# Value products of head pairs as quarters of the matmul array, in two banks that VectorE adds, under a new instruction order

## The chip, the cores and the metric

One core of a Trainium2 chip runs the whole program in one launch. The metric is the device time of one execution in microseconds (us). The kernel before takes 504.94 us, the median of three runs (504.84 to 505.65).

## What is computed

The reference, cut to what matters:

```python
# attention: 8 batches, 8 heads, 576 positions, 64 wide; window 128; bias by head
scores = scale * np.matmul(q, k.transpose(0, 1, 3, 2))
mask = (rel >= 0) & (rel < window)                  # rel = query - key
scores = np.where(mask, scores + bias[None], -1e9)
attn = softmax(scores);  attn_out = np.matmul(attn, v)
x = attn_out.transpose(0, 2, 1, 3).reshape(B, S, H * D)   # 512 wide
# four "experts", each a causal attention of its own on x, 64 wide
for e in range(4):
    q, k, v = x @ wq[e], x @ wk[e], x @ wv[e]
    a = softmax(causal(scale * (q @ k.transpose(0, 2, 1))))
    ye = a @ v @ wo[e]
    out += gate_weight(e)[..., None] * ye           # the two best of four by x @ w_gate
```

Only the product of the attention's probabilities with `v` is touched by the change. Because of the window, a key reaches only its own position and the 127 queries behind it.

## The kernel before, in words

The 576 positions are four blocks of 128 (`NQ` = 4, `P` = 128) and a tail of 64 (`TAIL`). The heads go in pairs: 32 pairs `g`, four to a batch, and a pair's results fill 128 partitions, head 0 in the lower 64 (`D` = 64) and head 1 in the upper. The work of one pair is: scores (`attn_s`, `products`), biased row minima on VectorE, exponentials on ScalarE, row sums and the scaling by them (`normalise`, on GpSimd or ScalarE), transposes of the probabilities on TensorE (`attn_t`), and the value product (`attn_pv`, `attn_pv_tail`). The first four pairs go through functions of their own (`half_s`, `half_t`, `half_pv`), which the change leaves as they are; `attn_pv` serves the other 28.

The transposed probabilities of a pair lie in one wide tile `ptT[g]`: keys on partitions, and for key block `c` and head `h` 256 columns, first the queries of the same block, then those of the next. `attn_pv(g, c)` multiplies the 128 keys of block `c` with these 256 columns (128 for the last block), one matmul for each head. A matmul whose weights have 128 rows and 64 columns takes half of the array, so the two heads run side by side. All four blocks add into one PSUM bank `x0`. Then the sum leaves PSUM in two parts, high and low:

```python
act_copy(xh[:, :512], x0, 512)                                  # ScalarE or VectorE, rounds to fp32r
dve_sub(xl[:, :512], x0, xh[:, :512].bitcast(F32), 512)         # VectorE
```

`attn_pv_tail` does the same for the 64 queries of the tail in a second bank `xt`. High and low part are the input `X` of the projections: `vproj` and `qkproj` multiply the four `X` of a batch with the high and low part of the weights, in fp32r on the whole array. The experts' attention (`moe_s`, `moe_t`, `moe_pv`, `moe_wo`) follows with up to a batch of delay. All this is interleaved.

A matmul on plain fp32 data (scores, value products) leaves two records in the trace, one for each of its two passes; fp32r matmuls and transposes leave one.

There are eight PSUM banks (`ps_s`, `ps_t` and `ps_a` are the same eight slots). `place` gives a tile a slot when the order reaches its first use, and frees it behind its last. Some instructions have two engines to choose from: `evac` (ScalarE or VectorE), `rnd` (GpSimd or ScalarE), `ssub` (VectorE or GpSimd).

Nothing is scheduled at run time. The functions only record instructions; `plan` then puts them in the order that the packed string `ORDER` holds (a place in the recorded list for each step, and which engine where there is a choice). Every engine works through its own part of that order from front to back, and waits at an instruction whose inputs or buffers are not ready. All instructions are issued by one line of the program, so the profile's rows are told apart by tiles: `ps` is a PSUM bank, `w` any of the SBUF slots, `wx` an `X`, `vt` the values, `WH`/`WL` the projection weights, `idt` the identity of a transpose.

Of the kernel before, what the change touches and what calls it, by code (L numbers as in the profile page):

```python
# [10 lines left out]
F32 = mybir.dt.float32  # L11
# [31 lines left out]
    "BWvdWi@@%Xnb!-wKJqVxw!OT_YgR2ElQ)qZaEB;BsZB33VcYTT6STbmv+d-p)GN4yYJ@6KY!)?`P1MqJ5^u(;*-Xnl5qv|=$U#8^b-)zmOs%^Qw63aUc"
    "m6ZVVA|YY{cmd|X2w+G6YgVAY(n{t)FnD>NLkGHrEV6}@5A+W70@~dJFTSOHga5up5Rw3wazMr~?-a(mge>7+?lSnQD$Bb}8a_5X5k&r2gc6W10>Iq8Z"
    "UzHrg{eRP4*ckaZ@&doVzCP*+wA6SgRW@(ZY+ea49J|-?x&U!{XOSe{&H{$R!iB(v>sn)pv4%NTT(p=A9+v{YaAW=7`%0Cj0H2g%|Pzu=Gc9uxsw^jvF"
    "Sz~cr6w%@&>JOu_V790C#+{0deut3fJHmKackDW9XWDss8DITToLnean`4+Q#b+scoIY{?fYD(ev^X>W|X--Sa<t(3EMm#b)qD4yT~!(}kvNK)@zKjK~"
    "|FDArC7#+T-K;ySX@(z^MaLc3|nUtqJ#7Fo>r2mkNEfBk_3O=@}LZmXlQ+?(gs-m4W1zasA*6v6yzP00j6_xi}4Js24ufzf#y8SPx<=zRsxYgXs{d{?l"
    "*ezf3k(^u63Tm_HzS#A%J7+kA>iaNnO#Ot9j*bkNEl?YE*)dJ`=+eaQR9|UOr47XUGUa^*x+|pQLgIl^=qn-hx&GuNdhCzR0P30;icXi>gUVsMNvLJ1J"
    "sCNHo4c1oxw4hsr>&y6T4X4J>&e)O~p;i!n#d&M_h1!wi)a0_-cet^lQP9(cbwk8xF~$Z+BQZl04@tZ5_&<x)bq~Gsu9{7<Kihr(U*8l4-T&~9WEMdE!"
    "-l54{pufoMelFA?T1EyrUoblD7dLF6ii=x_W&#z2rbZ;i-IA=QJZE@Ljb1H0ElJ92(?T^a<jjzV}B3MMh1$LeJ*RBIeGnh3Y71-;?uN=;+#>}lbN1r@X"  # L50
    "l3Brd7>P$9Zanut9@&019D94p~=0ZUHPsKna83{HH6YCszmDfm3m6-23o<davfY8_?Ab(1xLClV@21bkIr&WThlKJ-B=D<;#~YX~i+nk=lb7zmi^9bov"
    "+YzEH3trr$g`+A`@EM$X>+tJJKc^2JYI7R!wSsgGLLp#es7w|v!c=dDNTnYiO+5c~4slOWh$3eJsfSV$%8Wc~bp`;OLdbD6j-Lq+9RKC8*Kk<?;H(KzA"
# [194 lines left out]
def attn_moe_kernel(ctx, tc, hd, rd, vd, wall, wo, mk, tb, tm, mt, ident, out):  # L247
# [1034 lines left out]
```

## Time and profile before

| | |
|---|---|
| median of three runs | 504.94 us |
| the profiled execution's own time | 505.44 us |
| its span, first to last instruction | 503.6 us |
| TensorE busy / weight loads | 498.3 us (99%) / 428.3 us (85%) |
| VectorE, ScalarE, GpSimd busy | 420.0 us (83%), 352.5 us (70%), 178.2 us (35%) |
| DMA queue q1, share of the 16 engines | 31.8% |

The profiled execution lasts 1.8 us longer than its span. It is 0.5 us above the median of the three runs. "Busy" is the time in which at least one instruction of the engine is under way. Matmuls overlap each other, so TensorE's 99% does not say that each of its matmuls runs at the best rate; what a matmul costs is read from the distance of starts in the timeline.

### The profile page before, as it was taken

What the parts mean: (1) busy time and instruction counts of PE and PEld (TensorE: products, weight loads), DVE (VectorE), ACT (ScalarE), POOL (GpSimd) and SP (SyncE); (2) the same over time, 40 slices, a digit from 0 to 9 for tenths busy, and PEclk for the clock granted to TensorE, in tenths of its full rate; (3) what the DMA queues carried; (4) which work ended last, traced back from release to release, by engine and by line L of the source; (5) the groups of instructions that cost most, each with busy time, mean ns of one, the idle gap of its engine ahead of it and who ended that gap; (6) DMA issues with size and microseconds to landing.
All of it is one profiled execution on the core that took longest, in us unless ns stands there. A gap on an engine that the chain in (4) does not pass through costs nothing.

```text
span 503.6 us, 15006 instructions
## 1 busy us (share of the span) xinstructions
PE 498.3 (99%) x5212; PEld 428.3 (85%) x5212; DVE 420.0 (83%) x1879; ACT 352.5 (70%) x1313; POOL 178.2 (35%) x403
## 2 busy tenths in 40 slices
PE   8999999999999999999999999999999999999997
PEld 6888889897889879798887978989789897799775
DVE  5999999989995898968979899697988869845853
ACT  4969977887868478673797869556585878455852
POOL 3812425160715115252230603408152055105440
PEclk9999999999999999999999999999999999999999
DMA  7994440243107043054242312710344300200033
GB/s 202 281 233 123 105 109 3 65 110 99 38 17 197 13 122 97 6 147 123 68 114 72 81 53 61 214 33 1 87 134 143 81 2 1 91 1 1 2 105 126
DMA packets 29851, 44.83 MB, mean 89 GB/s; under 512 B 9424, under 2 KB 15824, under 8 KB 29776
## 3 DMA queue, kind: packets, MB, share of 16 engines
q1 hardware_dynamic: 29040, 43.42, 31.8%
q8 instruction: 41, 0.67, 0.6%
q10 hardware_dynamic: 736, 0.46, 0.4%
q14 instruction: 34, 0.28, 0.2%
HBM read 34.42 MB, written 9.44 MB: 87 GB/s over the span
## 4 chain that ended last, share of the span: by engine, by line
PE 98%; DMA 1%; SPq 0%; DVE 0%; issue 0%
PE ps L1194 98%; DMA w<-in_hd 1%; SPq L1194 0%; DVE w L1194 0%
## 5 line engine op out<-in xcount | busy, mean ns | idle before, releaser
L1194 POOL TENSOR_SCALAR w<-w,mr,w 128x256 f32<-128x256 f32 (+3 forms) x128 | 76.3, 606 | 111.4 <-DVE mr L1194 43.9
L1194 PE MATMUL ps<-wx,WH 128*128 128x288 f32 (+2 forms) x512 | 112.2, 300 | 0.0
L1194 ACT ACTIVATE w<-w,nm 128x128 f32<-128x128 f32 x252 | 98.6, 394 | 15.9 <-DVE nm L1194 14.8
L1194 ACT COPY w<-ps 128x512 f32<-128x512 f32 (+3 forms) x132 | 62.4, 499 | 41.5 <-PE ps L1194 32.1
L1194 POOL TENSOR_SCALAR w<-w,r 128x128 f32<-128x128 f32 x156 | 55.9, 369 | 92.7 <-DVE r L1194 29.7
L1194 PEld LDWEIGHTS ps<-wx,WH 128*128 128x128 f32 x512 | 83.2, 189 | 2.4 <-issue 0.9
L1194 ACT ACTIVATE w<-w,mnm 128x256 f32<-128x256 f32 (+3 forms) x128 | 70.8, 555 | 15.1 <-DVE mnm L1194 9.5
L1194 PE MATMUL ps<-idt,w 128*128 128x128 f32 x608 | 80.2, 276 | 0.0
L1194 DVE CUSTOM_DVE_ANT_0 w<-ps,tbt 128x128 f32<-128x128 f32 x288 | 72.5, 284 | 5.2 <-PE ps L1194 3.5
L1194 DVE TENSOR_TENSOR w<-ps,tmt 128x1024 f32<-128x1024 f32 (+2 forms) x96 | 71.6, 772 | 2.6 <-PE ps L1194 1.3
L1194 PEld LDWEIGHTS ps<-idt,w 128*128 128x128 f32 x608 | 69.0, 141 | 4.5 <-issue 1.3
L1194 PE MATMUL ps<-wx,WL 128*128 128x288 f32 (+2 forms) x256 | 71.8, 297 | 0.0
L1194 PE MATMUL ps<-w,vt 128*64 128x256 f32 (+2 forms) x784 | 66.1, 309 | 0.0
L1194 DVE COPY w<-ps 128x256 f32<-128x256 f32 (+3 forms) x90 | 47.7, 544 | 18.8 <-PE ps L1194 18.1
L1194 PE MATMUL ps<-WH,wx 128*128 128x260 f32 x288 | 62.3, 284 | 0.0
L1194 PEld LDWEIGHTS ps<-w,vt 128*64 128x64 f32 x784 | 44.2, 137 | 21.1 <-issue 3.5
L1194 PE MATMUL ps<-w 64*64 64x192 f32 (+2 forms) x1256 | 57.7, 313 | 0.3 <-DMA w<-in_hd 0.2
L1194 PEld LDWEIGHTS ps<-w 64*64 64x64 f32 (+1 forms) x1256 | 43.8, 138 | 10.3 <-issue 2.3
L1194 PE MATMUL ps<-w,w 128*64 128x64 f32 (+4 forms) x576 | 51.6, 318 | 0.0
L1194 DVE CUSTOM_DVE_ANT_0 w<-ps,mtt 128x384 f32<-128x384 f32 (+2 forms) x96 | 50.3, 551 | 0.9 <-PE ps L1194 0.5
L1194 DVE COPY_PREDICATED ps<-mkt,ps 128x256 f32<-128x256 int32 (+2 forms) x160 | 49.7, 329 | 1.1 <-PE ps L1194 0.5
L1194 ACT ACTIVATE w<-w,r 128x128 f32<-128x128 f32 x132 | 46.2, 395 | 5.3 <-DVE r L1194 5.1
(102 smaller groups left out, 933.1 us busy)
## 6 DMA issues: line engine op xcount, KB each, us to landing
w<-in_hd SPq DMA_DIRECT2D x56, 288.0 KB, 4.5
vt<-in_vd SPq DMA_DIRECT2D x28, 320.0 KB, 3.8
out<-w SPq DMA_DIRECT2D x31, 256.0 KB, 2.9
w<-in_hd SPq DMA_DIRECT2D x14, 128.0 KB, 4.0
w<-in_hd SPq DMA_DIRECT2D x56, 32.0 KB, 3.7
w<-in_wall SPq DMA_DIRECT2D x4, 386.0 KB, 5.3
out<-w SPq DMA_DIRECT2D x8, 128.0 KB, 2.4
vt<-in_vd SPq DMA_DIRECT2D x4, 192.0 KB, 4.1
```

The source lines that it names most:

```text
L1194: getattr(getattr(tc.nc, e), m)(*a, **k)
```

## The change

The value product of the 28 pairs is cut once more, by keys. `half(dst, q0, y, c, f, n)` takes the 64 lower (`y` = 0) or upper (`y` = 1) keys of block `c` and issues one matmul for each head, with weights of 64 rows and 64 columns, a quarter of the array. The 64 lower keys reach the first 192 of the 256 columns, the 64 upper keys the last 192, so each matmul has 192 columns in place of 256. Lower keys add into bank `xa`, upper keys into bank `ya`, and the tail's lower keys into a third bank `ta`; the tail's upper keys go into the first 64 columns of `ya`, which no other product uses.

The two banks are put together behind TensorE: `evac` copies `xa` to a tile `tmp` in SBUF, VectorE adds columns 64 to 511 of `ya` to it, `rnd` makes the high part from `tmp`, and `ssub` the low part, with no PSUM operand any more. For the tail, `evac` copies `ta` to a small tile and VectorE adds `ya`'s first 64 columns and writes the sum back to `ta`; `tail_out` is then what stood at the end of `attn_pv_tail`.

The string `ORDER` is replaced as a whole.

```diff
 ORDER = (
-    "c-obC4OAo7m1b4FD^<~|ZpoHnDG?qNix}AugDtXRjS|>EMjDG)$^jopAb|vCVJtFW!y0BG0Wa({4tOC0HXMTod0`C+%t8WVaOeciX%a|a3>$O;4xG@FW"
...
+    "c-obC0azr*b>?)}>#p9N*3L*X5@XF+j20wDfdm}Jh8Sc>zy}t{@C6dc!6&%D9oQfb7Mwr^8@wRF24ryHyf~~44#;5bN~{Go*bu=9EO0=9c=-%5_#lA`Y"
...
-    def attn_pv(g, c):
-        b, p = divmod(g, NP_)
-        vt = prepped[g][3]
-        if c == 0:
-            xacc[g] = ps_a.tile([P, 512], F32, tag="x" if K["X"] else "a", name=f"x{g}", bufs=K["X"] or K["A"])
-        x0 = xacc[g]
-        n = 2 * P if c < NQ - 1 else P
-        pc = ptT[g]
-        for h in range(2):
-            nc.tensor.matmul(
-                x0[D * h : D * h + D, P * c : P * c + n], vt[:, c, D * h : D * h + D],
-                pc[:, 4 * P * c + 2 * P * h : 4 * P * c + 2 * P * h + n],
-                start=(c == 0), stop=True, skip_group_check=True,
-            )
-        if c == NQ - 1:
-            X = xp.tile([P, 2 * S + TAIL], F32R, tag="xh", name=f"xh{g}")
-            xh, xl = X[:, :S], X[:, S + TAIL :]
-            xT[g] = (xh, xl)
-            xX[g] = X
-            act_copy(xh[:, :512], x0, 512)
-            dve_sub(xl[:, :512], x0, xh[:, :512].bitcast(F32), 512)
-            del xacc[g]
+    def attn_pv(g):
+        vt, pc = prepped[g][3], ptT[g]
+        xa, ya, ta = (ps_a.tile([P, 512], F32, tag="x", name=f"{n}{g}") for n in ("x", "y", "xt"))
+
+        def half(dst, q0, y, c, f, n, start=False):
+            r = slice(D * y, D * y + D)
+            for h in range(2):
+                m = 4 * P * c + 2 * P * h + f
+                nc.tensor.matmul(
+                    dst[D * h : D * h + D, q0 : q0 + n], vt[r, c, D * h : D * h + D], pc[r, m : m + n],
+                    start=start, stop=True, skip_group_check=True,
+                )
+
+        for c in range(NQ - 1):
+            half(xa, P * c, 0, c, 0, 3 * D, c == 0)
+            half(ya, P * c + D, 1, c, D, 3 * D, c == 0)
+        c = NQ - 1
+        half(xa, P * c, 0, c, 0, P)
+        half(ya, 0, 1, c, P, TAIL)
+        half(ta, 0, 0, c, P, TAIL, True)
+        half(ya, P * c + D, 1, c, D, D)
+        half(ta, 0, 0, NQ, 0, TAIL)
+        tmp = big2.tile([P, DM], F32, tag="xs", name=f"xs{g}")
+        evac(tmp, xa)
+        nc.vector.tensor_tensor(tmp[:, D:], tmp[:, D:], ya[:, D:], add)
+        X = xp.tile([P, 2 * S + TAIL], F32R, tag="xh", name=f"xh{g}")
+        xh, xl = X[:, :S], X[:, S + TAIL :]
+        xT[g], xX[g] = (xh, xl), X
+        rnd(xh[:, : NQ * P], tmp)
+        ssub(xl[:, : NQ * P], tmp, xh[:, : NQ * P].bitcast(F32))
+        tt = p2.tile([P, TAIL], F32, tag="xq", name=f"xq{g}")
+        evac(tt, ta[:, :TAIL])
+        nc.vector.tensor_tensor(ta[:, :TAIL], tt, ya[:, :TAIL], add)
+        tail_out(g, ta)
...
     def run(g):
         n = len(nc.ops)
-        for c in range(NQ):
-            attn_pv(g, c)
...
-        attn_pv_tail(g)
+        attn_pv(g)
```

What the new order does is shown at three places around pair 7, the last of its batch. The rows are in program order of one engine; `x2` counts matmuls that follow each other with equal text, and the sizes are those of the result (partitions x columns).

TensorE, the value product of pair 7 (`vt7`), before:

```order
L1194 MATMUL ps4_73<-w103_93,vt7_157 64x256 x6
L1194 MATMUL ps7_76<-w103_93,vt7_157 64x64 x2
L1194 MATMUL ps4_73<-w103_93,vt7_157 64x128 x2
L1194 MATMUL ps7_76<-w103_93,vt7_157 64x64 x2
L1194 MATMUL ps0_69<-w50_82 64x192 x2
L1194 MATMUL ps2_71<-w50_82 64x192 x2
```

and now:

```order
L1206 MATMUL ps5_74<-w103_93,vt7_158 64x192 x2
L1206 MATMUL ps4_73<-w103_93,vt7_158 64x192 x2
L1206 MATMUL ps5_74<-w103_93,vt7_158 64x128 x2
L1206 MATMUL ps4_73<-w103_93,vt7_158 64x64 x2
L1206 MATMUL ps0_69<-w103_93,vt7_158 64x64 x2
L1206 MATMUL ps4_73<-w103_93,vt7_158 64x64 x2
L1206 MATMUL ps0_69<-w103_93,vt7_158 64x64 x2
L1206 MATMUL ps2_71<-w57_89 64x128 x2
L1206 MATMUL ps7_76<-w57_89 64x128 x2
```

The first two of these rows are the last of three equal pairs. Twelve matmuls in two banks became 22 in three (`xa` is `ps5`, `ya` is `ps4`, `ta` is `ps0`); behind them the scores of another pair follow at both times.

TensorE, the first projection that reads the `X` of pair 7 (`wx3` before), before, ten rows on from the last row of the product:

```order
L1194 MATMUL ps0_69<-w50_82 64x192 x2
L1194 MATMUL ps2_71<-w50_82 64x192 x2
L1194 MATMUL ps3_72<-wx0_77,WH_109 128x288
L1194 MATMUL ps4_73<-wx4_81,WH_109 128x288 x2
L1194 MATMUL ps4_73<-wx4_81,WL_110 128x288
L1194 MATMUL ps4_73<-wx1_78,WH_109 128x288
L1194 MATMUL ps3_72<-wx0_77,WL_110 128x288
L1194 MATMUL ps3_72<-wx3_80,WH_109 128x288 x2
```

and now (pair 7 is `wx2`):

```order
L1206 MATMUL ps5_74<-w57_89 64x192 x2
L1206 MATMUL ps4_73<-wx4_81,WH_109 128x288
L1206 MATMUL ps6_75<-wx1_78,WH_109 128x288
L1206 MATMUL ps4_73<-wx4_81,WH_109 128x288
L1206 MATMUL ps4_73<-wx4_81,WL_110 128x288
L1206 MATMUL ps4_73<-wx0_77,WH_109 128x288 x2
L1206 MATMUL ps4_73<-wx0_77,WL_110 128x288
L1206 MATMUL ps4_73<-wx1_78,WH_109 128x288
L1206 MATMUL ps6_75<-wx1_78,WL_110 128x288
L1206 MATMUL ps4_73<-wx1_78,WH_109 128x288
L1206 MATMUL ps6_75<-wx2_79,WH_109 128x288
```

Between the scores and the first read of pair 7 there stood six projection matmuls; now there are ten.

GpSimd, the same stretch of the program, before:

```order
L1194 TENSOR_SCALAR QJm_118<-QLm_122 64x64
L1194 TENSOR_TENSOR w0_145<-ex_117,ws0_170 128x5x4
L1194 TENSOR_SCALAR w53_85<-w53_85,mr0_0_0_171,w0_145 128x256
L1194 TENSOR_SCALAR MPL0_119<-MPL0_119,mr0_0_2_174 128x576
L1194 TENSOR_SCALAR QJm_118<-QHm_121 64x64
```

and now:

```order
L1206 TENSOR_SCALAR QJm_118<-QLm_122 64x64
L1206 TENSOR_SCALAR w54_86<-w54_86,r7_0_167 128x128 x2
L1206 TENSOR_TENSOR wx0_77<-w22_96,wx0_77 128x512
L1206 TENSOR_SCALAR wx1_78<-w23_97 128x512
L1206 TENSOR_TENSOR ex_117<-lg0_144,mx0_172 128x5x4
L1206 TENSOR_TENSOR wx1_78<-w23_97,wx1_78 128x512
L1206 TENSOR_TENSOR w0_145<-ex_117,ws0_173 128x5x4
L1206 TENSOR_SCALAR QJm_118<-QHm_121 64x64
L1206 TENSOR_SCALAR w50_82<-w50_82,mr0_0_0_174,w0_145 128x384
L1206 TENSOR_SCALAR w50_82<-w50_82,mr0_0_0_174,w0_145 128x128
L1206 TENSOR_TENSOR wx2_79<-w24_98,wx2_79 128x512
```

The subtractions (`TENSOR_TENSOR wx`) and some of the roundings (`TENSOR_SCALAR wx`) of the `X` now stand on GpSimd between the gates and the scaling of the probabilities; pair 7's low part is the last row.

## Rows read from the trace of the kernel before

**Rows 1.** The page: busy times, the granted clock, and the chain that ended last.
```profile
PE 498.3 (99%) x5212; PEld 428.3 (85%) x5212; DVE 420.0 (83%) x1879; ACT 352.5 (70%) x1313; POOL 178.2 (35%) x403
...
PEclk9999999999999999999999999999999999999999
...
PE ps L1194 98%; DMA w<-in_hd 1%; SPq L1194 0%; DVE w L1194 0%
```

**Rows 2.** Waits of the weight loads: releaser: us in total, times, longest us.
```profile
PEld ps L1194 <- issue: 22.2, 101, 0.5
```

**Rows 3.** Timeline of TensorE, value products as halves (start, us, ..., xrecords).
```profile
419.22 1.03 PE L1194 MATMUL ps<-w,vt 128*64 128x256 f32 x8
420.08 0.60 PE L1194 MATMUL ps<-w,w 128*64 128x256 f32 x4
...
89.78 0.39 PE L1194 MATMUL ps<-w,vt 128*64 128x128 f32 x4
90.00 0.49 PE L1194 MATMUL ps<-w,w 128*64 128x384 f32 x2
...
437.25 0.29 PE L1194 MATMUL ps<-w,vt 128*64 128x64 f32 x4
437.37 0.72 PE L1194 MATMUL ps<-w,w 128*64 128x64 f32 x8
```

**Rows 4.** Timeline of TensorE, scores as quarters, and what follows.
```profile
327.50 0.98 PE L1194 MATMUL ps<-w 64*64 64x128 f32 x24
328.42 0.77 PE L1194 MATMUL ps<-w,w 128*64 128x64 f32 x6
...
355.44 1.63 PE L1194 MATMUL ps<-w 64*64 64x128 f32 x40
357.00 0.65 PE L1194 MATMUL ps<-w,w 128*64 128x512 f32 x2
```

**Rows 5.** Timeline of TensorE, a value product ahead of a change of shape.
```profile
136.21 0.39 PE L1194 MATMUL ps<-w,vt 128*64 128x128 f32 x4
136.53 0.98 PE L1194 MATMUL ps<-w 64*64 64x128 f32 x24
```

**Rows 6.** Groups by form: xcount | busy us, mean ns | idle before.
```profile
L1194 DVE TENSOR_TENSOR wx<-ps,wx 128x512 fp32r<-128x512 f32 x28 | 19.2, 686 | 1.7 <-ACT wx L1194 1.6
L1194 DVE COPY w<-ps 128x384 f32<-128x384 f32 x22 | 12.0, 550 | 2.7 <-PE ps L1194 2.3
L1194 DVE CAST wx<-ps 128x64 fp32r<-128x64 f32 x10 | 2.1, 219 | 1.8 <-PE ps L1194 1.7
L1194 ACT COPY w<-ps 128x512 f32<-128x512 f32 x66 | 37.4, 586 | 11.4 <-PE ps L1194 10.9
L1194 POOL TENSOR_TENSOR WL<-w,WH 128x772 fp32r<-128x772 f32 x4 | 7.4, 1848 | 1.0 <-ACT WH L1194 0.8
L1194 POOL TENSOR_SCALAR WH<-w 128x772 fp32r<-128x772 f32 x2 | 1.7, 835 | 0.0
```

**Rows 7.** Busy time by stretch: PE, PEld, DVE, ACT, POOL, clock, DMA share, GB/s.
```profile
40.00:60.00 20.00, 20.00 (x267) 17.26 (x258) 19.48 (x101) 17.91 (x76) 9.56 (x21) 1.00 0.33 89
60.00:80.00 20.00, 20.00 (x203) 17.71 (x200) 19.58 (x89) 15.82 (x69) 6.94 (x19) 1.00 0.37 102
80.00:100.00 20.00, 20.00 (x224) 16.98 (x223) 19.37 (x90) 14.75 (x58) 4.61 (x10) 1.00 0.17 42
```

**Rows 8.** Timeline around the value product of pair 7 and its X.
```profile
71.26 1.97 PE L1194 MATMUL ps<-w,vt 128*64 128x256 f32 x24
...
73.15 1.63 PE L1194 MATMUL ps<-w 64*64 64x192 f32 x40
...
73.88 0.69 DVE L1194 TENSOR_TENSOR wx<-ps,wx 128x512 fp32r<-128x512 f32 x1
...
75.49 0.29 PE L1194 MATMUL ps<-wx,WL 128*128 128x288 f32 x1
75.62 0.42 PE L1194 MATMUL ps<-wx,WH 128*128 128x288 f32 x2
```

More of the change, by code (lines that the diff above doesn't have):

```diff
@@ L43 @@
[L43 to L52, printed above, removed]
@@ L113 @@
[L113 to L115 removed]
+    "c-obC0azr*b>?)}>#p9N*3L*X5@XF+j20wDfdm}Jh8Sc>zy}t{@C6dc!6&%D9oQfb7Mwr^8@wRF24ryHyf~~44#;5bN~{Go*bu=9EO0=9c=-%5_#lA`Y"
+    "k?1xMP95$;$Btv48yLH^YyYY(_LNt>ec`L|9@=|41e(ZhI98Ae8+vNmAXIy7$2Fu32;Lhu^TA_huRAv5jvnED!{5*%tmW)LUu-?H7dTUxo<97u`8D;bu"
@@ new lines @@
+    "_Ml%}BQrjQDY1efJG85ye;q>NuXb1z;}!(ciRpcDyLdXYxpy>M2f!Jjhdwaq{b_2YW{}&stS(iLgJV5c;YmYD<3COw~RmH|tPQX0K1v8(rD$OUp}}wm|"
+    "@>!2ca84UMo`Y#ECwP!ID-aILc)I;P6-Y1Ple4@+j@zkK6iLR3@h8_G{a7leex!{;8dKPoo0?h%p#+3rS|hdG>SDZ4WTh5-%-p*9*u<`heC=w%u@J2e|"
+    "s*f1W`V1-2(vs^s?h-4-=jHwAEiW+H8T*Huw8dV60NC$RQLKSIiPF{ilqD)NJ-R!g};b4CLd*A*7b+;Rpu(-sy+J?NsG~-R>Y7E8&Dqv0t1OV&?!lg-1"
+    "rV`PZoS77FwTGzPo(j;84rs@HST_?2HL!Tg+LW3Z<#N!Nf<`l5O%K5Z5?e4NCq&i+S-@&qgN$r|9LR-|ZBO6iOw34HXE4-7PL6fnHWW6e*_{z2slu*A#"
+    "5r8bMe9!vHeE`B5(7ah?T>dBn{o;X?Tw{P1w9FaEsiCH#bC(=$g|>yA{wKZ0~{*_kVMR#zk=XE(P~o9+P?&80QnYYQEEtRR&uyItx*p?cH$5kt+4>xm="
@@ new lines @@
+    ">pnI9ebEVxzRH!R%K!K=m4|?-f^U%U?>jgaqXkhnZ>%75Bn?<p2DDrKs7VIv;;DKBdm`W#faEvkx>-OQ<`=p$zg#Qdu5DFgvx7x-yfWQye-sIt?rycEn"
+    "aH&V=ldtA>J2P}cI&qp~lLj|?Y69A1JL#R#`^b1*uHf*ydu_=J}4mcIDx8+#GPvV|+=LKqvIoSG!}e$_^jauREb1~O)c__Rwfv)orgJD?1x;xW$`t<na"
+    "Y#S&(jR@Rj@YF0CFYoN5K6kxN$v$Y<&TfSO!-@~+U&)jD2+E~4`!Dg9(+4%75HBcPTSGzQ|l=azj?J+IoRV5XHxg+^Xxkc?LFD*B(!<h#<GU*G?QKzB1"
+    "k3W8BbZ9gZCYx&jx4CP)r7S%9h@G#^WWTReCIX*7GMW9VR`$0m&V8xUqxKCQ1+GnA`o@=`s1K}p%fkQpi2K>W!NN2+8yWfpR9c&8V?db67C3jmbY!khP"
+    "Rp!Vn7^*xGQ4zOxw%Fy^+c!`bFG>R1EAJn!VwmZI(&xRkz2l>(L&1<dx@HxaoA{aG_<uc>;fb~1T;IT#YOE(zDjeU((R;O2Ym0rsO{1rtXDyKuq&FXd1"
@@ new lines @@
+    "00WC2JI1c|`5IZGbj__P})UFP1Ex8;330@L~3A8T6`y+bV?+*fsA&#4hg-TVDQZtb73qHydW4WvdDzx7N4T0lH_W048gP;Wms-mKMP%WQ0ci@+{D&-W|"
+    "C%KL${k$C3$9Pz>)!e&O%lOsVpG{F$QC#y?J!Zyl_`LNpvV_PRnNLUwP`!`Hq=_pe^M)q$X{D<=*6S(ye3ri9#*XWuIsPg*Kd%5$UQbDR*S*anMNDoV1"
+    "WLZ={13wXjEGP|>3o|*5qH^FZE_HO)5Q|gYxlNht>IWU7lZoyxQCTrYMD@NoXD=<GZ539G;)eY$9Gjy&P7iO1j3d?S91FYmgZz2R*T??}#O;)A5r6kmh"
+    "I4A|I!OaDwk{a_b+aQpZ28Lz!<`?bL*{OM@nFQh8xSG;x1Dg|pI@45Cb~rXU_VgRI5#t5N#Ra9dV(U9r<ttzR%Q{Q-WIXhO0eZRs3s{~0^!tR`EJO)WY"
+    "3x05uYo%h2_E3SUn)k$P_3-(Y^|?t*0pzHbq{zN8m(hadr$S&X846KPs4=OXr2#z>F<>p8hye8GqgrIdh0(`!mD4ly#CV5%1=6B;VALeeu?}^V^C{y*$"
@@ new lines @@
+    "ScKBeN0roGmDwS!^dA@g#b3<nJF(VE1|s-}wzR1M(h9N`4MNc1D<G0ES8C)h~(#PrYugt{py<f9}vAgE4_C$khsEjsUnv42GkH#I|POoN+C<GB?9S>q;"
+    "Y|Lyb28c3=Ulb{CEL?L!b67-rd#MVw_jEB>G)=vsSKbMH}f%9wi9Hg>4qo?QTHbnIJ+f~9fcSFny%$gqdCxXGSdb}1E7I+5vN1@VZr`O1GSzG}K+?Nes"
+    "q+)u7Ra@P50;cR$TTh?c*FPv+h#aaU<#0UVar1hareDLn}e(OMQ+x9M2&K^|5*3JfT(`IvPRZjjTvr!@9WALT~fOK%Y@#4Q;1&3v5`vAu6PF8EmG0en9"
+    "sgO)^vg6)=xu<8_m|bv7iH4-YnZn=Rc=XJ<@N9B8J~jxA4Jq3+?y#;tJv%-rV7B8Q|JM=Sc~5q<SJ?8>rO(+)n=807KxkBK7zA4IQy7X5!$893#b?5rh"
+    "ra)dR@7tYxm4<DU=%&T&>9$Kq9zA?SM2AT#n$k%e>PWxl~NlhnLBGqxv-~rEEaz8fqV03k<MQIbXx>uB_zj2D!Eggkr7jL?_j+!zZw}ECOLRfPi8OAMM"
@@ new lines @@
+    "hZC>uc)c(v#<n?|gpja45B+knCrq7lfqt%|sv#v5kNHvC-k{?Jdx`K7L*deCum0s*e)&Z}IQ+#0ql6?BPw8y%}oz^;7kZx=LeHZ3{I{!Q>pQ99Kh|^NK"
+    "p~cNa`qMyM)8PGOV*MWyRo;9*J*+NQ}*B>nJ7O@QQY4^C%Q+}drL9E0J(Tw`l?e{xsWHF^AnackV_Kvz*s$Z%Ir*9~3nkD)VT^$4tSKYV=*28i;l2m7P"
+    "8@H|51iysSmDiXd8&8^YUe|35S2FqY#X<-Sk#(mLwu4`<geRSN@Ps4++^o5QE=ee$wm6b$vRnn@D|8VGPZ2#iiA^@tmJtNzJGS+#FhN8NO6@-}%>;%;y"
+    "`O-3@wHaCz&%BlKD=&aL9@mSHyZ-4ndrEYW)t*+Evs6M3MwtHqJHLvugy`(Lf&fqNuRo?+bD7ihx-$*ly5H8K^eVBivDy<KzHc;l!5ECLAR*u8H_k2If"
+    "F*tDISH^(nAZj?w^pD1co>RToVvShgrB|vzC*VaaLM7SSnYuSw)2UVn=hVkzWAm4jLH{AUj0sA_xyPg%dMkm9NZ<AAX4E7@?6L{Y$vZj{8u&YyYOe}0j"
@@ new lines @@
+    "XliW8b4@b1V&Cqggct**W=i{rP9&&7XNVEcyE4%y^E|P&A%$P+8a5GFfh$TF9)O9g0|MjgN9a^yz_}<NEfJQCFO;JH2?WVH{(bn*HU2fH+-eC?DT(-?F"
+    "RgSEpu`^{uHy3d(>tb}VEVZi2=ZT*OXUe_LnZQ{Sm?>akQ==_Tf^u7)V~f`<4xSc9Mbb*r<gys8{xjvy*N^hQc+eu5IZPrv`Q(S$V$L`g_d%BdTI<nz&"
+    "(@e~+jZm}8;l9mG-rV5M8E3c)v8VmpUjl7Dtf>iQ=LT-cIY|l4YVFCtvOL5=F(nq5j-oCfJ!D=M55)N<(jmU341RMdVjw6!;rS_EcAN+X4Wp~;gP;I%i"
+    "sSuM@AsT0+6t{Zn8dd=UyUg;-B~?S6{U3-P`9I^<t}U;HGKwA9SY_+#Uxbi(bS}N25q;f#Nz<^=mjuap$peXTiLkn{x{*{r+~D3^2-rP1{==UIIPGsf-"
+    "*mGu2f`wAjltQ_JwG-6gU>(rd+#h6{xq#@dg7=AT*}n!vHaWPh{$?cURM?Fo-&3XR3^ypN51(<<T`dBJckm7lg;R#abxQ0S~FHWl>vvhgU^4j6i;-gEK"
@@ L116 @@
+    "FL2%Q1b>9?!aXL1eEzWFMsN^oD*f<V5ewB;wT+V(`9y^}bgSxO-sw!1q#bXLRM!tcKPGGqZ$0GV3v@ti4z>e8{_39k~216h4iIWkwU;Zu_(n`n?7{c_*"
+    "aFr9o?G4dU<enp*f>-e&)<@4){r|9i3^"
 )
@@ L631, in attn_pv_tail, with tail_out @@
                 )
+        tail_out(g, xt)
+    def tail_out(g, xt):
         xh, xl = xT[g]
@@ L981, in run @@
         n = len(nc.ops)
-        for c in range(NQ):
-            attn_pv(g, c)
-        if K["gr"] == 2:
-            nc.alt["runs"].append([i for i in range(n, len(nc.ops)) if nc.ops[i][0] == "tensor"])
-        attn_pv_tail(g)
+        attn_pv(g)
         for _ in range(K["rn"]):
```

112 lines of the change are left out of this document (45 added, 67 removed).

## The prediction

> **What bounds the kernel now.** I read the page first. TensorE is busy 99% of the span at the full granted clock, and the chain that ended last runs over TensorE's own instructions for 98% of it [rows 1]. So nothing but TensorE's line of work sets the end, and a busy TensorE can still be waiting between two matmuls. The waits of the weight loads settle that: the largest entry by far is 22.2 us in 101 short pieces for "issue", which is no other engine [rows 2]. TensorE's line is dense; only less or cheaper work on it makes the kernel shorter, and any new wait on it makes it longer at once. What a matmul costs I take from the distance of starts in the timeline, not from its duration, since matmuls overlap.
>
> **The value product.** Halves: eight records of 256 columns start at 419.22 and the next work of the same shape at 420.08, so one record costs 0.86 / 8 = 0.1075 us [rows 3]. A pair has three blocks of 256 columns, two heads, two passes: 12 records, 1.29 us. Quarters do not occur with values, but the scores already run as quarters, 192 columns wide, with the two row halves in two banks, as the change does it. Two score runs that both end ahead of a half-array product differ by 16 records of 192 columns: 1.56 us against 0.92 us [rows 4], so 0.64 / 16 = 0.040 us each. The pair now has 24 such records: 0.96 us. That is 0.33 us less for each of 28 pairs, **9.2 us**.
>
> The rest of the pair gains nothing. Block 3 had four records of 128 columns, 0.22 us, and the tail eight of 64 columns, 0.12 us for four [rows 3]: together 0.46 us. As quarters, block 3's 128 lower columns run beside 64 upper ones and last as long as the longer, and the tail still takes two turns of 64 columns, in one of which both row halves work. I take 0.46 us again. Quarters of 64 columns alone stand in no row: from below, they cost what a turn of halves costs; from above, each record starts no closer than the cheapest one shown, 0.03 us, so that four quarters cost 0.12 us a pass where halves cost 0.06. With two passes in one such group, and 0.01 us more a pass in block 3, that is 0.14 us a pair, up to 3.9 us. I take zero, because 0.040 us for 192 columns is half of what halves take for as many (0.1075 x 192 / 256 = 0.081), so quarters do run four abreast.
>
> **Changes of shape.** The array works whole, as halves or as quarters. The same four records of 128 columns take 0.22 us when more of their shape follows [rows 3] and 0.32 us when quarters follow [rows 5]: a change costs 0.10 us. Counted over the order, TensorE changes its shape 127 times before and 116 times now, since value products can stand beside scores without one. Eleven fewer: **1.1 us**.
>
> **What is added elsewhere.** On VectorE the 28 subtractions from PSUM go (0.686 us each). In come 28 additions of 448 columns, between the 0.550 of 384 and the 0.686 of 512 columns, about 0.62; 28 small additions and 15 small copies of 64 columns, 0.22 each [rows 6]. That is 0.27 us more a pair, 7.5 us in all, less a few copies that the order hands to ScalarE: some 5 us on 420. ScalarE takes those copies, about 12 us on 352. GpSimd takes 27 subtractions of 512 columns: 1848 ns for 772 columns [rows 6] make 1.23 us each, 33 us; and 21 roundings, 835 ns for 772 columns, 0.55 us each, 12 us. With 45 us more on 178, GpSimd stays under half busy. All of this lies beside TensorE, which covers it as long as no result comes late. SyncE issues the same DMAs as before (241 instructions in its part of either order) in a somewhat different order, and I count them at nothing, between minus and plus 1 us, since TensorE's whole wait for a load is about 1% of the chain [rows 1].
>
> **The sum.** 9.2 + 1.1 = 10.3 us off the profiled execution's 505.44 us gives 495.1; it ran 0.5 us above the median of the runs, so I forecast **494.6 us**. From no change a measurement of this kernel can tell about 0.2%, 1 us.
>
> **What is late next.** The path from the last value product to a finished X grows. Before: one evacuation (0.586) and one subtraction (0.686) [rows 6], 1.27 us; for pair 7 the trace has the next work at 73.15 and the subtraction's end at 74.57 [rows 8]. Now: evacuation 0.586, addition 0.62, rounding 0.55, subtraction on GpSimd 1.23: 3.0 us, **1.7 us longer**. Banks are also held longer: three in place of two, and `ya` from the first quarter until VectorE's addition. At pair 7, the order before leaves between the product's end and the first read of its X: half a tail (0.12), 40 score records (1.56 with the change of shape) [rows 4] and six projection matmuls of 0.13 [rows 8], 2.5 us for a path of 1.3. The new order leaves 0.12 + 1.56 + 10 x 0.13 = 3.0 us for a path of 3.0, and the high part, read first, is there after 1.8. So it just fits; the cover grew by less than the path.
>
> **Rivals.**
>
> *X comes late and TensorE waits (slower).* GpSimd works in order, and the subtraction of pair 7 now stands behind gates, roundings and scalings of other tiles, as the order of GpSimd shows. If the 1.7 us are exposed once for each of the seven batches that use the new path, that is 12 us: **506.6 us**. It decides from 10.3 / 7 = 1.5 us a batch. For it: TensorE has no slack, and at pair 7 no margin. Against it: the other pairs of a batch are read much later than their own product, GpSimd is idle for two thirds of the time, and the order now has four more projections ahead of the read. Chance 0.08.
>
> *VectorE bounds one stretch.* From 40 to 100 us VectorE is busy 58.43 us of 60 [rows 7], and five pairs have their product there. TensorE's stretch would shrink by 5 x 0.33 = 1.65 us, to 58.35, while VectorE needs 58.43 + 5 x 0.27 = 59.8 us, if no copies are moved off it: 1.5 us of the gain lost, **496.1 us**, and 498 if late additions hold banks as long elsewhere. For it: that stretch has no air. Against it: the order gives more of the copies to ScalarE, which is busy only 48.5 us there. Chance 0.15. The Trainium skill, in "TensorEngine Tiling (Array Packing)", section PSUM Bottleneck, warns of just this: tiling speeds up TensorE and not the evacuation of PSUM, which can then become the bound. By that rule alone the stretch would be VectorE's; the row shows it short of that by 1.57 us.
>
> *Small records have a floor.* If four quarters of 64 columns cannot start faster than 0.03 us each, 3.9 us come back: **498.5 us**. For it: 280 more matmuls, 560 more records. Against it: the 0.040 us at 192 columns. Chance 0.10. The Trainium skill speaks for it: "TensorEngine Tiling (Array Packing)", section Instruction Overhead, states about 60 cycles of overhead for each matmul and the same time for 1 column as for 60. An estimate by that page, at 2.4 GHz, is 25 ns for each of 560 records, 14 us, which would leave the kernel slower by 4 us; no row here shows such a sum, as the 192-column records stand at 40 ns with streaming included.
>
> *The row halves do not run side by side.* Then a record of 192 columns costs 0.1075 x 192 / 256 = 0.081 us, 24 of them 1.94 us, 18 us more over 28 pairs: **521.9 us**. The scores speak against it [rows 4]. Chance 0.02.
>
> **Chances and range.** The forecast, give or take 1.5 us, has 0.57; the rest (0.08) is a gain larger than the sum, where the new order also has fewer of the short waits. Faster by over 0.2%: forecast, larger gain, VectorE, floor, less a little: 0.88. Within 0.2%: 0.03, where several small losses meet. Slower: 0.09. The range goes from 493.0 (1.6 us of waits saved) to 499.5, which takes in the floor and VectorE's stretch with 1 us for DMAs; about 0.15 lies outside.
>
> **What will show it.** Right: `w,vt` records of 192 columns on 64x64, 672 of them, at 0.040 us in the timeline; VectorE's additions near 0.62 us; GpSimd's subtractions near 1.2 us; TensorE still 99% busy in a span about 10 us shorter. X late: weight loads that wait for GpSimd's or ScalarE's `wx`, longer than 0.5 us. VectorE's stretch: waits for VectorE's `ps` between 40 and 100 us. A floor: 64-column records on 64x64 at 0.03 us and more. The forecast is wrong if the value products cost over 1.6 us a pair, or TensorE's waits grow by over 3 us.

## The result, and the profile after

The changed kernel takes 498.24 us, the median of four runs (497.45 to 500.16), against 505.12 us for the kernel before (504.84 to 505.65): a ratio of 0.9868, with an interval from 0.9839 to 0.9897. The gain is 6.9 us, or 1.3%. The forecast was 494.6 us and its range 493.0 to 499.5: direction and range held, and a third of the forecast gain did not come. The profiled execution took 497.45 us, 8.0 us less than the one before.

The page of the changed kernel, for [rows 1]:

```profile
span 495.4 us, 16247 instructions
...
PE 487.4 (98%) x5772; PEld 430.7 (87%) x5772; DVE 421.3 (85%) x1918; ACT 359.3 (73%) x1349; POOL 222.5 (45%) x440
...
PE ps L1206 69%; DVE w L1206 1%; DVE ps L1206 0%; ACT AHm L1206 0%; DVE ALTm L1206 0%; DVE nm L1206 0%; DVE ALm L1206 0%; DVE mr L1206 0%
```

VectorE is hardly busier (1.3 us, forecast 5), ScalarE by 7 us (forecast 12), GpSimd by 44 us (45). The chain is followed back only to 144.8 us here, so its 69% is not a share of TensorE that fell. Of the 347 us that it covers, TensorE has all but about 6, most of them in one stretch of VectorE and ScalarE from 324 to 329 us. What its weight loads waited for, for [rows 2] (releaser: us in total, times, longest us):

```profile
PEld ps L1206 <- issue: 21.6, 98, 0.4
...
PEld ps L1206 <- DMA w<-in_hd: 2.3, 6, 1.0
```

The value product of pair 7 and the scores behind it, for [rows 8], in the timeline of TensorE (start, us, ..., x records):

```profile
69.33 1.58 PE L1206 MATMUL ps<-w,vt 64*64 64x192 f32 x42
70.71 0.33 PE L1206 MATMUL ps<-w 64*64 64x128 f32 x2
70.75 0.23 PE L1206 MATMUL ps<-w,vt 64*64 64x64 f32 x2
70.81 1.58 PE L1206 MATMUL ps<-w 64*64 64x128 f32 x38
72.39 0.67 PE L1206 MATMUL ps<-wx,WH 128*128 128x288 f32 x3
```

Its 44 records and two of the scores take 70.81 - 69.33 = 1.48 us. Before, the product's 24 records and one change of shape took 73.15 - 71.26 = 1.89 us [rows 8]. The instructions added elsewhere, for [rows 6] (x count, busy us, mean ns, idle before):

```profile
L1206 DVE TENSOR_TENSOR w<-w,ps 128x448 f32<-128x448 f32 x28 | 17.0, 608 | 0.2
L1206 DVE TENSOR_TENSOR ps<-xq,ps 128x64 f32<-128x64 f32 x28 | 6.3, 223 | 0.3
L1206 POOL TENSOR_TENSOR wx<-w,wx 128x512 fp32r<-128x512 f32 x27 | 34.7, 1287 | 1.1
L1206 POOL TENSOR_SCALAR wx<-w 128x512 fp32r<-128x512 f32 x21 | 13.0, 619 | 32.0 <-DVE w L1206 26.7 <-PE ps L1206 5.2
```

Busy times from 40 to 100 us, for [rows 7]:

```profile
40.00:60.00 20.00, 20.00 (x319) 18.69 (x312) 19.90 (x104) 18.20 (x80) 11.19 (x21) 1.00 0.68 155
60.00:80.00 20.00, 20.00 (x248) 18.72 (x247) 19.12 (x93) 17.05 (x71) 15.11 (x33) 1.00 0.34 92
80.00:100.00 20.00, 19.98 (x246) 17.71 (x245) 17.95 (x93) 17.09 (x65) 5.73 (x12) 1.00 0.03 6
```

VectorE is full in the first of them (19.90 of 20 us), and TensorE is still busy throughout. The one large wait of TensorE behind the start-up is elsewhere, at pair 10:

```profile
114.97 1.10 PE L1206 MATMUL ps<-w 64*64 64x128 f32 x24
116.57 0.56 PE L1206 MATMUL ps<-w,vt 64*64 64x192 f32 x8 [0.50 <-DMA vt<-in_vd]
```

The first value product of pair 10 waits for its values. From the records ahead of it to its own start there are 0.68 us too many; without them it would start at 115.9 us. In the kernel before, the same load and the same product stand like this:

```profile
111.04 0.33 SPq L1194 DMA_DIRECT2D vt<-in_vd  x1
```

```profile
118.73 1.73 PE L1194 MATMUL ps<-w,vt 128*64 128x256 f32 x16
```

How long the load takes, before, after, and in the second trace of the changed kernel below (KB, us from issue to landing):

```profile
vt<-in_vd SPq DMA_DIRECT2D x1, 320.0 KB, 4.6
vt<-in_vd SPq DMA_DIRECT2D x1, 320.0 KB, 5.9
vt<-in_vd SPq DMA_DIRECT2D x1, 320.0 KB, 7.3
```

So the values used to be there at 115.7 us, 3.0 us ahead of their product.

**Where TensorE's time went.** The table sums the distance from each matmul record to the next, by what the first of the two is, from the first projection to the last matmul (18.05 to 499.63 us before, 17.86 to 491.37 us after), in us. The last three columns are kernels of the experiments.

| | before | after | again | wide256 | vt10_act |
|---|---|---|---|---|---|
| value products, with a change of shape behind them | 57.84 | 49.07 | 49.35 | 57.61 | 49.15 |
| changes of shape behind other work | 22.00 | 21.07 | 21.06 | 20.86 | 21.29 |
| everything else, waits included | 401.75 | 403.38 | 404.65 | 401.56 | 402.61 |
| sum | 481.59 | 473.52 | 475.06 | 480.03 | 473.05 |

The two upper lines fell by 9.7 us, near the forecast's 10.3. The third line, where the instructions are the same, rose by 1.6 us: TensorE waits there.

### The profile page after: what moved, and what is told of

Its sections match the earlier page's. It is cut to its first block, busy times and chain, and to the rows that moved or that the text cites. A ratio compares the mean times of both kernels' runs of the same rounds, so it can differ in the third digit from the quotient of the medians.

```text
span 495.4 us, 16247 instructions
## 1 busy us (share of the span) xinstructions
PE 487.4 (98%) x5772; PEld 430.7 (87%) x5772; DVE 421.3 (85%) x1918; ACT 359.3 (73%) x1349; POOL 222.5 (45%) x440
## 4 chain that ended last, share of the span: by engine, by line
PE 69%; DVE 1%; issue 0%; ACT 0%
PE ps L1206 69%; DVE w L1206 1%; DVE ps L1206 0%; ACT AHm L1206 0%; DVE ALTm L1206 0%; DVE nm L1206 0%; DVE ALm L1206 0%; DVE mr L1206 0%
## 5 line engine op out<-in xcount | busy, mean ns | idle before, releaser
L1206 ACT COPY w<-ps 128x512 f32<-128x512 f32 (+3 forms) x165 | 78.7, 504 | 49.3 <-PE ps L1206 42.7
L1206 POOL TENSOR_SCALAR w<-w,mr,w 128x512 f32<-128x512 f32 (+3 forms) x128 | 76.4, 609 | 74.5 <-DVE mr L1206 50.8
L1206 ACT ACTIVATE w<-w,mnm 128x128 f32<-128x128 f32 (+3 forms) x128 | 70.9, 556 | 14.5 <-DVE mnm L1206 12.7
L1206 DVE TENSOR_TENSOR w<-ps,tmt 128x256 f32<-128x256 f32 (+2 forms) x96 | 71.2, 771 | 2.8 <-PE ps L1206 2.4
L1206 PE MATMUL ps<-w 64*64 64x192 f32 (+3 forms) x1256 | 59.8, 306 | 2.1 <-DVE ps L1206 1.3
L1206 PE MATMUL ps<-w,vt 64*64 64x192 f32 (+4 forms) x1344 | 57.2, 284 | 0.5 <-DMA vt<-in_vd 0.5
L1206 DVE COPY w<-ps 128x512 f32<-128x512 f32 (+3 forms) x85 | 47.5, 565 | 9.2 <-PE ps L1206 8.6
L1206 PEld LDWEIGHTS ps<-w,vt 64*64 64x64 f32 (+1 forms) x1344 | 48.9, 133 | 6.7 <-issue 1.0
L1206 ACT ACTIVATE w<-w,r 128x128 f32<-128x128 f32 x137 | 48.4, 396 | 5.1 <-DVE r L1206 4.9
L1206 PE MATMUL ps<-w,w 128*64 128x64 f32 (+4 forms) x576 | 48.2, 319 | 0.1
```

Of the source, the lines that this page charges most:

```text
L1206: getattr(getattr(tc.nc, e), m)(*a, **k)
```

## Experiments

**The changed kernel again.** No edit.

> The changed kernel once more, unaltered. First theory: what keeps its median 0.8 us above its own profiled execution (498.24 against 497.45 us) is TensorE's clock, granted at 1.2 GHz for a few microseconds in some executions, behind a wait that the kernel before does not have. Then the times go with the mean granted clock again: about 0.5 us more for each 0.001 less, 497.3 us at 0.999 and 500.2 at 0.993, the median 498.2 give or take 0.5, and a trace with a mean below 0.999 shows one stretch at 1.2 GHz that begins behind a wait. Rival: the clock falls anywhere, without a wait ahead of it, and as often in the kernel before.

498.34 us, median of four (497.48 to 499.13), ratio 0.9865 (0.985 to 0.9879). The first theory fell. In these four executions the times do not go with the mean granted clock: 499.13 us at 0.997, 498.52 at 0.995, 498.15 at 0.996, 497.48 at 0.997; and the kernel before ranged from 0.992 to 1.0 too. (Of the first four executions the longest, 500.16 us, had the lowest mean, 0.993; it has no trace, so a lower clock behind a wait is not ruled out there.) In this trace (that of the 499.13 us) the clock is lower in one stretch only, in the start-up, which lasts until the loads are there at either clock (the first projection starts at 18.02 us, against 17.86 us in the trace with no such stretch). Busy time and clock of TensorE there:

```profile
5.00:10.00 5.00, 3.47 (x56) 0.99 0.88 224
10.00:15.00 5.00, 4.97 (x49) 0.67 0.94 304
```

TensorE was busy for only 3.47 of the 5 us before the stretch with a mean of 0.67. What differs is the wait for the values of pair 10:

```profile
115.01 1.10 PE L1206 MATMUL ps<-w 64*64 64x128 f32 x24
117.95 0.56 PE L1206 MATMUL ps<-w,vt 64*64 64x192 f32 x8 [1.84 <-DMA vt<-in_vd]
```

It is 2.03 us here, 1.35 more than in the other trace, of a difference of 1.68 us between the two executions. The new theory is this wait. SyncE's issues of loads, same trace:

```profile
91.03 19.40 SPq L1206 DMA_DIRECT2D w<-in_hd  x8
110.53 0.53 SPq L1206 DMA_DIRECT2D vt<-in_vd  x1
111.10 5.63 SPq L1206 DMA_DIRECT2D w<-in_hd  x7
```

Within the first row SyncE stands still from 92.83 to 107.21 us. In the program's order the load at its front goes into a slot (`w50`) that the experts' probabilities hold until TensorE has read the last of them for its transposes, just ahead of 107.2 us. Then SyncE issues a load about every 0.65 us, five ahead of the values and seven behind them. The kernel before has such a stop too, up to 106.99 us, and also five loads between it and these values. In both traces the values were issued at 110.5 us and used the moment they came: once at 116.57, once at 117.95.

**The narrowing undone.**

```diff
-            half(xa, P * c, 0, c, 0, 3 * D, c == 0)
-            half(ya, P * c + D, 1, c, D, 3 * D, c == 0)
+            half(xa, P * c, 0, c, 0, 4 * D, c == 0)
+            half(ya, P * c, 1, c, 0, 4 * D, c == 0)
```

> The changed kernel with the narrowing undone: each quarter of blocks 0 to 2 takes all 256 columns of its block, whose other 64 hold zeros; order, banks, additions and everything else stay. First theory: the gain is the 64 columns that a quarter leaves out, 0.0107 us for each of 24 records and 28 pairs at the measured rate (0.0537 against 0.0414 us a record gives 8.3 us, the forecast's 0.33 us a pair 9.2 us), so 506.5 to 507.5 us, no better than the kernel before. Rival: the new order gives the gain, and the time stays below 501 us.

504.84 us, ratio 0.9996 (0.9985 to 1.0006): the gain is gone, 6.5 us of it. Pair 7 in its timeline:

```profile
70.85 1.90 PE L1206 MATMUL ps<-w,vt 64*64 64x256 f32 x42
72.54 0.33 PE L1206 MATMUL ps<-w 64*64 64x128 f32 x2
72.58 0.23 PE L1206 MATMUL ps<-w,vt 64*64 64x64 f32 x2
72.64 1.58 PE L1206 MATMUL ps<-w 64*64 64x128 f32 x38
```

72.64 - 70.85 = 1.79 us against 1.48: 0.31 us for the pair, the forecast's 0.33. Over all pairs the value products take 8.3 us more than in the run above (57.61 against 49.35). The time is 6.5 us longer, not 8.3, because the waits shrink when the products are slower (401.56 against 404.65 in the third line, as in the kernel before). So the gain is the columns left out, and 2 to 3 us of it come back as waits. The new order with quarters of full width brings nothing that these runs can tell (504.84 against 505.00 us), though in the trace TensorE's line is 1.6 us shorter than before (480.03 against 481.59); that execution's start-up was 0.7 us longer.

**Quarters in the order before.** Ten pairs at first; the whole product stands where its first matmul stood, the rest as the expectation says.

> The kernel before in its own order, with the value product of ten pairs as quarters (4, 6, 9, 11, 17, 20, 21, 23, 24, 25: those for which that order has a third PSUM bank and an SBUF slot free); their matmuls stand where the first of the old ones stood, the addition, rounding and subtraction where evacuation and subtraction stood. First theory: each pair gains its 0.33 us by itself, 3.3 us for ten, so 501.8 us give or take 0.7. Rival: without the new order the longer path to X and the third bank cost as much as they gain, and the time is 504.5 us or more.

526.34 us, ratio 1.0419 (1.0403 to 1.0434). In this kernel the copies of a tail can stand ahead of the product, so parts of the tails of ten pairs' X are left out. Then with each piece at the place of its counterpart, and with the starting flag set by the order:

```diff
-        sw[id(mm[0])] = new
+            sw[id(mm[2 * c])] = list(nc.ops)
...
+        sw[id(mm[6])] = list(nc.ops)
...
+        sw[id(mm[8])] = list(nc.ops)
...
+        sw[id(mm[10])] = list(nc.ops)
...
+            kw["start"] = w not in seen
```

> The kernel before in its own order, with the value product of eleven pairs as quarters (4, 6, 9, 11, 17, 19, 20, 21, 23, 24, 25, for which a third bank is free), now with every piece of the product where its counterpart stood. First theory: the old order has no cover for the longer path to X and for banks held longer, and TensorE waits on VectorE at many places: over 510 us, as with ten pairs (526.34 us). Rival: those waits came from putting the whole product at the place of its first matmul, and each pair now gains its 0.33 us: 501.4 us give or take 1.

> The eleven pairs in the order before once more; the flag that starts the upper keys' bank now stands on whichever of its matmuls comes first in that order (in the run before it stood on block 0 always, so that a tail taken first was left out). Nothing else differs, so 529.6 us give or take 1.5. Rival: the flag had a part in the waits, and the time falls towards 501.

529.58 us (1.0483, 1.0458 to 1.0507) and 530.28 us (1.049, 1.0471 to 1.0508). Neither the placing nor the flag brought the time down. In the order before, eleven pairs as quarters make the kernel 25 us slower, where their matmuls alone would save 3.6. The weight loads of the last one wait, for VectorE above all:

```profile
PEld ps L1293 <- DVE ps L1293: 9.0, 13, 2.1
PEld ps L1293 <- DVE mnm L1293: 5.4, 15, 1.2
PEld ps L1293 <- ACT w L1293: 5.3, 11, 1.1
```

The same three rows read 1.0, 2.9 and 2.4 us in the kernel before. They make up 13 of the 25 us, and they are waits for banks and for softmax work; for X (`POOL wx`) the weight loads wait 0.4 us in all. The array also changes its shape 144 times from the first projection on, against 118 before; at the forecast's 0.10 us that is 2.6 us. A third bank for each pair also shifts which bank every later tile gets. How much each of these costs was not separated, so the cause of the 25 us stays open in part.

**The values of pair 10 issued earlier.** First by SyncE itself, right behind pair 8's product (`d` and `m` are that DMA and pair 8's last matmul):

```diff
+    d, m = nc.alt["vt"][10], nc.alt["pv"][8]
+    seq_ = [o for q in seq_ if q is not d for o in ((q, d) if q is m else (q,))]
```

> The changed kernel with one DMA moved: SyncE issues the values of pair 10 right behind the value product of pair 8, whose buffer they take, ahead of loads of q and k that wait for 19 us. First theory: the wait of 0.68 us at 115.7 us goes and the clock that falls behind it in some executions stays up: 497.5 us or less, every mean granted clock 0.998 or above. Rival: the wait goes (0.7 us) but the clock falls as before, about 0.996 in most executions; or the other loads come 1 us later and the wait moves.

500.37 us, ratio 0.9916 (0.99 to 0.9932): slower than the changed kernel. I had read pair 8's product at 88 us as whole. The order cuts it, as the order before did: in the changed kernel 32 of its records run from 88.31 us, the last 12 from 107.17, and only then is its buffer free. SyncE, which works in order, waits for that, here until 108.40 us. Four loads of `q` and `k` that had gone out between 71 and 93 us now stand behind it, and a load of them or behind them, late now, stops TensorE:

```profile
122.64 0.43 PE L1210 MATMUL ps<-w 64*64 64x128 f32 x6 [2.70 <-DMA w<-in_hd]
```

```profile
120.00:125.00 5.00, 2.37 (x15) 0.91 0.69 190
125.00:130.00 5.00, 5.00 (x21) 0.75 0.00 0
```

(The second fence has stretches of TensorE: busy, count, granted clock, DMA share, GB/s.) Behind a wait of 2.70 us the granted clock falls to 0.75 of full speed as a mean of 5 us, part of it at 1.2 GHz; the output projections of 512 columns, otherwise 0.23 us apart, start 0.43 us apart there. TensorE's line in this trace is 4.1 us longer than in the next kernel's (477.18 against 473.05 us), of which the wait is 2.9 by the distance of starts; so it cost 1.2 us more than itself.

Then by ScalarE, whose queue is not held up, at the same place:

```diff
+        if g == 10:
+            nc.scalar.dma_start(vt, vd[b, p])
```

> The changed kernel with one DMA moved: the values of pair 10 are issued by ScalarE, right behind the value product of pair 8, whose buffer they take, in place of SyncE behind seven other loads. First theory: the wait at 115.7 us (0.68 us in one trace, 2.03 us in the other) is SyncE's queue, which stands still for 14 us and then issues one load each 0.65 us; the values come earlier, the wait goes, and the median falls by 0.7 to 2 us to 496.3 to 497.6 us. Rival: the 16 DMA engines are full there, another load comes as much later, and the time stays at 498.3 give or take 0.5.

> The kernel whose values of pair 10 are issued by ScalarE, unaltered, on another occasion. First theory: the gain over the changed kernel is real, 1.5 us: 496.8 us give or take 0.4, a ratio of 0.984 to the kernel before. Rival: it was the luck of few executions, and the ratio comes out at 0.9865 as for the changed kernel.

496.79 us, ratio 0.984 (0.9827 to 0.9854), and on the second occasion 496.47 us, ratio 0.9828 (0.9811 to 0.9844). This is faster than both kernels, and 1.5 to 1.9 us faster than the changed one. The issue, and TensorE at the same place as above:

```profile
107.42 0.33 ACTq L1213 DMA_DIRECT2D vt<-in_vd  x1
```

```profile
114.72 1.10 PE L1213 MATMUL ps<-w 64*64 64x128 f32 x24
115.64 0.51 PE L1213 MATMUL ps<-w,vt 64*64 64x192 f32 x8
```

The values are issued 3.1 us earlier and the wait is gone. The three traces hold the same matmuls; behind the start-up, the start of this product is the only distance from one to the next that is longer in the changed kernel by more than 0.3 us (0.68 and 2.02). The Trainium skill, "DMA: Bandwidth & Descriptors", section Rules for kernel authors, says that spreading DMAs over issuing engines brings no bandwidth and saves only the sequencer's issue time; the runs agree: what the values gained is the time that SyncE needs to issue the five loads ahead of them.

**How near is the next limit?** Four kernels: VectorE's addition left out, the same addition twice, the subtraction twice, and the subtraction on VectorE.

```diff
     seq_ = plan(nc.ops, nc.alt) if K["mode"] else nc.ops
+    seq_ = [o for o in seq_ if not any(o is c for c in nc.alt['cut'])]
...
+    seq_ = [o for q in seq_ for o in [q] * (2 if any(q is c for c in nc.alt['cut']) else 1)]
...
         ssub(xl[:, : NQ * P], tmp, xh[:, : NQ * P].bitcast(F32))
+        nc.alt[len(nc.ops) - 1][1] = nc.alt[len(nc.ops) - 1][0]
```

`cut` holds the additions, or the subtractions; the first added line leaves them out, the second issues them twice, and the third gives every subtraction to VectorE.

> The changed kernel without VectorE's 28 additions of the upper keys' bank (448 columns, 17.0 us in all); the upper keys' share of these columns is left out of the result. First theory: VectorE's work is hidden behind TensorE, 498.3 us give or take 0.5. Rival of the forecast, VectorE bounds a stretch: 1.5 us less or more, 496.8 us or below.

497.65 us, ratio 0.986 (0.9841 to 0.9878), not to be told from the changed kernel. The wait for pair 10's values is in this trace too, and it is longer, 1.7 us by the distance of starts:

```profile
PE ps L1208 <- DMA vt<-in_vd: 1.6, 1, 1.6
```

From 40 to 100 us, where the rival had VectorE as the bound, TensorE's line is as long as with the addition, to 0.2 us: the rival fell. Its whole line (the sum of the table) is 473.34 us, and 471.6 without that wait, against 472.8 for the changed kernel without its own. VectorE's addition costs about 1 us in all.

> The changed kernel with every subtraction that makes the low part of X issued twice, so that the low part comes 1.29 us later on GpSimd (27 of 28), and GpSimd has 35 us more to do. If the forecast's working is right, that the path to the last X of a batch just fits its cover, TensorE waits 1.3 us in each of the seven batches: 507 us, and at least 502 us. Rival: the cover is larger than the forecast worked out, or GpSimd's part is not on the path, and the time stays at 498.3 give or take 0.7.

517.44 us, ratio 1.0249 (1.0235 to 1.0263): 19 us more, not 9. Waits of TensorE's weight loads, then one of the places, on TensorE and on GpSimd:

```profile
PEld ps L1208 <- POOL wx L1208: 12.1, 10, 2.6
...
PEld ps L1208 <- POOL w L1208: 4.2, 6, 1.6
```

```profile
327.67 0.53 PE L1208 MATMUL ps<-wx,WH 128*128 128x288 f32 x2 [2.33 <-POOL wx L1208]
```

```profile
325.00 2.61 POOL L1208 TENSOR_TENSOR wx<-w,wx 128x512 fp32r<-128x512 f32 x2
```

X is late at ten places and not at seven, and what stands behind the subtractions on GpSimd, the scaling of probabilities (`w`), is late as well. In the changed kernel no wait for `POOL wx` is among TensorE's: the path to X fits, with less than 1.3 us to spare at these places. Each doubled subtraction delays X and also keeps GpSimd busy; the run does not separate the two.

> The changed kernel with each of VectorE's 28 additions issued twice (the upper keys' sum is so added twice to the result): VectorE has 17 us more to do, and every X comes 0.61 us later. First theory, after the doubled subtraction cost 19 us: X has next to no margin, whichever engine delays it, so 0.61 us more on each costs about 0.61 / 1.29 of that, some 9 us: 505 to 509 us. Rival: it was GpSimd's queue, where other work stands behind the subtractions; VectorE has room, and the time stays at 498.3 give or take 0.8.

511.64 us, ratio 1.0131 (1.0108 to 1.0155), 13 us more for 17 us of VectorE's work:

```profile
PEld ps L1208 <- DVE w L1208: 9.8, 20, 1.1
```

This row reads 2.1 us in the changed kernel. The reason in the first theory does not hold: X (`POOL wx`) is late at one place, by 0.5 us. The price comes in short waits for VectorE's results of all kinds (`w`), at twenty places.

> The changed kernel with all 28 subtractions on VectorE (27 come from GpSimd, which loses 35 us; VectorE gains some 17 to 19 us, at 0.61 to 0.69 us each). First theory: VectorE is the tighter engine from 40 to 100 us, where it has hardly any idle time, and TensorE waits for it there: 500 us or more. Rival: X is finished 0.6 us earlier and GpSimd's queue is free, so nothing is lost or a little gained: 498.5 us or less.

514.46 us, ratio 1.0182 (1.0162 to 1.0203). One subtraction takes 712 ns on VectorE against 1287 on GpSimd, and still the kernel loses 16 us:

```profile
PE ps L1207 <- DVE wx L1207: 5.6, 3, 4.0
```

```profile
60.00:80.00 20.00, 15.87 (x205) 13.88 (x206) 19.66 (x87) 16.36 (x69) 9.32 (x23) 0.95 0.42 110
```

From 60 to 80 us TensorE is busy for 15.87 us of 20 and VectorE for 19.66: X is late because VectorE has no time to make it. The forecast's rival of VectorE as the bound is real one step further on: taking 17 us off VectorE gains about 1 us, adding 17 to 20 us costs 13 to 16.

## Why the prediction was right, and what it missed

- **The range held, the forecast itself did not.** 494.6 us give or take 1.5, to which I gave 0.57, misses 498.24. The range takes it in because it was drawn wide for a floor and for VectorE's stretch; neither came, and about half of what is missing comes from a term that I had put at nothing. To that extent the hit of the range is luck. What the gain is made of was right, as follows.
- **Value product: right, a little too cheap.** Forecast 9.2 us, measured 8.8 with the changes of shape behind the products. The 672 records of 192 columns take 27.80 us in the trace after, 0.0414 us each, where I took 0.040 from the scores: 24 x 28 x 0.0014 = 0.9 us.
- **Block 3 and the tail: right.** With the mean of all such records, before 112 x 66.6 ns + 224 x 32.8 ns = 14.8 us, after 448 records of 64 columns and 112 of 128: 13.3 + 1.6 = 14.9 us. A record of 64 columns stands at 29.8 ns, just the floor that I gave as the upper bound, and there are twice as many; but the 112 of 128 columns beside them cost 14.3 ns each in place of 66.6, and nothing is lost. The Trainium skill's rule ("TensorEngine Tiling (Array Packing)", section Instruction Overhead), which by my estimate made 14 us of it, is not what these runs show: its fixed cost is not paid in series by records of different quarters.
- **Changes of shape: right.** 116 stand in the trace, 127 before. Behind other work than value products they fell from 22.00 to 21.07 us.
- **Work elsewhere: right.** 0.608 us for the addition (forecast 0.62), 0.223 (0.22), 1.287 (1.23), 0.619 (0.55). Leaving the addition out changes the time by about 1 us.
- **"It just fits": right,** and the most useful sentence of the forecast: 1.29 us more on X and on GpSimd costs 19 us. In the order before, the change is 25 us slower with eleven pairs; but there the waits are for banks and softmax work, so that run does not show what the path to X would cost. I gave the rival in which X comes late a chance of 0.08 and priced it at 12 us for seven batches. The place was right and the price too low: there are ten places, and GpSimd's other work is late too.
- **The step that failed: "SyncE issues the same DMAs as before ... and I count them at nothing, between minus and plus 1 us".** The number of DMAs is the same, and SyncE issues the values of pair 10 at nearly the same time: at 111.04 us before, at 110.49 now. What moved is TensorE, which could start on them at 115.9 us in place of 118.73, and the landing, 5.9 and 7.3 us after the issue in place of 4.6. The 3.0 us by which the load used to be early are gone, and TensorE waits 0.68 or 2.03 us. The reason that I gave for "nothing" does not bear on this: the 1% of the chain in [rows 1] is the first load of the program, which lands at 6.9 us, and it says nothing of how early the later loads come. Of the 1.6 us by which the third line of the table rose in one trace this wait is 0.68, of the 2.9 us in the other it is 2.03; the other 0.9 us are short waits that were not traced to a cause. The wait for pair 10's values differs from one execution to the next, which would explain why the median gained 6.9 us and the profiled execution 8.0; the executions without a trace do not show it. With this one DMA on another queue the kernel is 8 to 9 us faster than before. Four other gaps of 0.17 to 0.33 us in the second trace, at 146, 177, 240 and 330 us, were not pursued.

## What to carry to other kernels

When the bounding engine is made faster, ask each queue that feeds it how early it can run: a load that came 3 us early is late now, and neither a count of DMAs nor the chain that ended last shows it. Compare when each load lands with when its reader starts. See what the front instruction of such a queue waits for, and how many loads stand behind it; a load that is short of issue time can go to another engine's queue. And test the margin by adding work, not only by removing it: here leaving out VectorE's addition gained about 1 us, and more work on VectorE or GpSimd cost 13 to 19 us.

## What the runs showed of the hardware that I had not expected

- The same load, issued at 110.49 us in one execution and 110.53 in another, let the waiting product start at 116.57 and at 117.95 us. Its landing is reported in 16 parts: 15 had come by 115.56 and 115.81 us, the last at 116.43 and 117.82. TensorE waited for one part of sixteen; why that part was late is not shown.
- On GpSimd a subtraction of 512 columns takes 1287 ns and on VectorE 712 ns, and the kernel is 16 us faster with the slower one: what counted was whose time was free.
- A wait of 2.70 us on TensorE was followed by a stretch at the lower clock (0.75 as a mean of 5 us), and one of 2.03 us was not (1.00 from 115 to 125 us).
